# Two 2 MB stores of split weights become eight of 0.5 MB, moved from the attention of batch 0 to the steps beside the MoE block

## The chip, the cores and the metric

The kernel runs on one core of one Trainium2 chip. Time is device time in microseconds (us) of one execution, lower is better. The profile shown comes from one execution taken by the hardware profiler. The engines are PE (matrix multiply, with PEld for its weight loads), DVE (vector), ACT (scalar), POOL (GpSimd) and SP (sync). Two of them, SP and ACT, issue the DMA transfers here, each through a queue of its own: q1 in the profile is SP's, q10 is ACT's. Sixteen DMA engines carry the packets of both queues.

## The reference

Three stages run on x of shape (2, 768, 512), all in float32:

```python
# attention, B=2, H=8, S=768, D=64, with a mask from 6 hash bits
mask   = q_bucket[:, :, :, None] == k_bucket[:, :, None, :]
scores = where(mask, scale * q @ k.T, -1e9)
x      = softmax(scores) @ v                   # heads side by side: (2, 768, 512)
# gated block ("MoE")
h      = maximum(x @ w_in, 0);  u, v = h[..., :512], h[..., 512:]
v_n    = (v - mean(v)) / sqrt(var(v) + 1e-6)
v_s    = einsum('ts,bsd->btd', w_spatial, v_n) + b_spatial[None, :, None]
x      = (u * v_s) @ w_out
# channel block
xn     = (x - mean(x)) / sqrt(var(x) + 1e-6) * g_ln
out    = x + maximum(xn @ w_ch1, 0) @ w_ch2
```

`w_in`, `w_out`, `w_ch1` and `w_ch2` come as 64-bit floats and are converted on the chip. Float32 products are made of three passes over two parts, a rounded one and its remainder, so each weight is kept as a pair of arrays.

## The kernel before

The program is not written in the order in which it runs. Every operation is added to a list (class `Plan`). A planner then estimates a cost for each, lays them out by engine and by due time, and only then issues them. Each engine, and each queue of issued transfers, works in the order that came out of it. The line numbers in the profile are therefore almost all those of the one line that issues (L499); operations are told apart by their tiles.

**Attention.** There are 96 steps, one for each query tile of 128 rows: 2 batches x 8 heads x 6 tiles, so head 6 begins at step 36, head 8 (the first of batch 1) at step 48, head 10 at step 60, head 12 at step 72 and head 14 at step 84. A step makes scores (`sc`, PE), the masked maximum (`x<-sc`, DVE), the exponentials (`x<-x,nb`, ACT) and transposes (`pt`, PE, copied to `e`). After a head the weighted sum follows (`po`, 24 matmuls). The scores of a head read `ks`, which is put together from the split keys by five small transfers on SP's queue (`ks<-k` three times, `ks<-m` twice); `qs` is built in the same way for every three tiles. `ks` has two buffers, so that of one head is filled during the head before it.

**MoE block.** `moe1(0)` starts at step 60 (`M0`) and is spread over the steps to 96, 24 pieces in all; `moe1(1)` follows after the attention. The block's weights `v` and `u` (the two halves of `w_in`) and `out` are converted during the attention: `CONV_AT` gives the steps, four pieces of 0.5 MB for each weight. A piece is loaded (`f_v`, `f_u`, `f_out` on ACT's queue), turned from 64-bit words into a float on ACT, DVE and POOL, and split into the tile of its weight (2 MB, 16 KB a partition). The tiles of `v` and `u` stay on the chip until batch 0 of the block has used them. Then their room is taken, by `out` and by the second load of `v`. So both are also stored to `w_split` in memory, and read back for batch 1 by `reload` (`w_v<-ws_v`, `w_u<-ws_u`, SP). The stores run on ACT's queue. `out` is stored in eight pieces of 256 KB as it is split (`ws_out<-w_out`) and read by both batches.

**Later steps.** From step 71 on, eleven pieces of `w_ch1` are converted and kept in memory as well (`KEPT_AT`, tiles `f_w`, `f64c_w`, `kept`). Columns of `w_spatial` are loaded (`wst_sp`, SP) and split (`w_sp`) for the block's spatial product (`pg`), whose result, gated (`gt`) and transposed (`ptr_g`), goes into the product with `out` (`py`).

Functions in `conv_steps` are called with `plan.soon` set: the planner may place such an operation as soon as PE has come within 55 entries of it in the list, without regard to when it is due. Transfers are ordered by what they read and write, tile part by tile part, and the reuse of a tile waits for all that used it.

Of the kernel before, what the change touches and what calls it, by code (L numbers as in the profile page):

```python
# [9 lines left out]
F32 = mybir.dt.float32  # L10
# [494 lines left out]
def attn_moe_kernel(ctx: ExitStack, tc: tile.TileContext, qT, kT, v, proj, w_in, w_spT, b_sp, w_out, g_ln, w1, w2, out):  # L505
# [3 lines left out]
    nc = plan = Plan(tc)  # L509
# [15 lines left out]
    CB = 2  # L525
    CONV_AT = (5, 11, 18, 24, 31, 37, 44, 50, 58, 62, 66, 70)
    CONV_D = (-1, 0, 3, 3)
    KEPT = (6, 8, 10, 12, 14, 0, 1, 2, 3, 4, 5)
    KEPT_AT = (72, 75, 78, 81, 84, 86, 88, 90, 92, 94, 95)
    QA = 3  # L530
# [16 lines left out]
    KFT = DM // P  # L547
# [20 lines left out]
    def stage_f64(src, nm):  # L568
        a, n = src.shape[1], src.shape[2]
        st = pools["conv"].tile([P, a, n, 2], U32, tag="f64", name=f"f64_{nm}")  # L570
        nc.scalar.dma_start(out=st, in_=src)
        return st

    def words_f64(st, nm):

        a, n = st.shape[1], st.shape[2]
        lo, hi = st[:, :, :, 0], st[:, :, :, 1]
        c = pools["conv"].tile([P, a, n], U32, tag="f64c", name=f"f64c_{nm}")
        cf = c.bitcast(F32)
        nc.scalar.activation(cf, hi.bitcast(F32), AF.Abs)  # L580
        nc.vector.tensor_scalar(cf, cf, F64_MIN, F64_MAX, op0=ALU.max, op1=ALU.min)
        nc.vector.tensor_scalar(c, c, 3, 0x3FFFFFFF, op0=ALU.logical_shift_left, op1=ALU.bitwise_and)
        nc.vector.scalar_tensor_tensor(hi, hi, 0xC0000000, c, op0=ALU.bitwise_and, op1=ALU.bitwise_or)
        nc.vector.tensor_scalar(c, hi, 0xFF800000, None, op0=ALU.bitwise_and)
        nc.vector.scalar_tensor_tensor(cf, lo, 2.0**-52, cf, op0=ALU.mult, op1=ALU.mult)
        return hi.bitcast(F32), cf

    def join_f64(tf, cf):
        nc.gpsimd.tensor_tensor(cf, tf, cf, op=ALU.add)
        return cf  # L590
# [382 lines left out]
    w_split = {}  # L973
    wp = {}
    moe_w = []

    def converted(src, dst, nm, after=None):

        d = {}

        def stage():
            d["st"] = stage_f64(src, nm)

        def words():
            d["tc"] = words_f64(d["st"], nm)

        def join():
            d["f"] = join_f64(*d["tc"])

        def finish():  # L990
            to = dst()
            split_f64(to[0], to[1], d["f"].rearrange("p a n -> p (a n)"))
            after(to)

        return stage, words, join, finish

    def moe_tile(key, b):
        pool = mp if len(moe_w) % 2 else keep
        wp[key, b] = pool.tile([P, 2, KFT, HF], F32R, tag="w", name=f"w_{key}_{b}", bufs=1)
        moe_w.append(wp[key, b])  # L1000
        return wp[key, b]

    def conversions():

        res = []
        for key, src, at in (("v", w_in, HF), ("u", w_in, 0), ("out", w_out, 0)):
            w_split[key] = dram.tile([P, 2, KFT, HF], F32, tag=f"ws_{key}", name=f"ws_{key}")
            for k in range(KFT):

                def dst(key=key, k=k):  # L1010
                    if key == "out":
                        parts = [
                            mp.tile([P, NKT * P], F32R, tag=f"sp{i}", name=f"w_out_{k}_{i}", bufs=2 - i) for i in range(2)
                        ]
                        return [x[:, :HF] for x in parts]
                    if k == 0:
                        wp[key] = moe_tile(key, 0)
                    return [wp[key][:, i, k] for i in range(2)]

                def after(to, key=key, k=k):  # L1020
                    if key == "out":
                        for i in range(2):
                            nc.scalar.dma_start(out=w_split[key][:, i, k], in_=to[i].bitcast(F32))
                    elif k == KFT - 1:
                        nc.scalar.dma_start(out=w_split[key], in_=wp.pop(key).bitcast(F32))

                src_k = src[:, k : k + 1, at : at + HF]
                res.append(converted(src_k, dst, f"{key}_{k}", after))
        return res
# [152 lines left out]
    conv_steps = {}  # L1182
    for at, stages in zip(CONV_AT, convs):
        for delay, e in zip(CONV_D, stages):
            conv_steps.setdefault(at + delay, []).append(e)
    kept = {}
    for n, f in enumerate(KEPT):
        d = {}

        def kept_words(f=f, d=d):  # L1190
            d["tc"] = words_f64(d["st"], f"w1_{f}")

        def kept_join(f=f, d=d):
            kept[f] = dram.tile([P, KFT, P], F32, tag=f"kept{f}", name=f"kept_{f}")
            nc.scalar.dma_start(out=kept[f], in_=join_f64(*d["tc"]))

        def kept_stage(f=f, d=d):
            d["st"] = stage_f64(w1[:, :, f * P : (f + 1) * P], f"w1_{f}")

        for delay, e in zip(CONV_D, (kept_stage, kept_words, kept_join)):  # L1200
            conv_steps.setdefault(KEPT_AT[n] + delay, []).append(e)
    m0 = None
    n0 = 0
    for i in range(-1 - QA, NT + PO + 3):
# [449 lines left out]
```

## Time and profile before

| | |
|---|---|
| median of 3 runs | 660.97 us (659.72 to 661.21) |
| the profiled execution, own time | 658.13 us |
| its span, first to last instruction | 656.1 us |
| PE busy | 639.9 us (98%) |
| DVE, ACT, POOL busy | 503.1, 326.7, 218.1 us |
| mean granted TensorE clock | 0.995 |
| bytes moved by DMA | 107.68 MB in 60962 packets |

The span lies inside the execution's own time, with 2.0 us around it. PE is the engine with the most work. A time of one instruction in the timelines is its start and its length; square brackets give how long the engine stood idle before it and what ended that.

### The profile page before, as it was taken

The numbers are of one execution on the slowest core, as the hardware profiler recorded it, in microseconds if no ns is written. First come the engines' busy times: TensorE is split into PE (matmuls) and PEld (weight loads), VectorE is DVE, ScalarE is ACT, GpSimd is POOL, SyncE is SP. The second block draws the span as 40 slices with busy tenths as digits, with TensorE's granted clock in tenths as the row PEclk, the third lists the DMA queues.
The fourth block names the chain that finished last, engine by engine and source line by source line (L and its number), as shares of the span: only waits on it lengthen the run. The fifth ranks groups of instructions, "written<-read, shape, count | busy, mean of one in ns | idle before, by whom it ended". The sixth has DMA issues, their size and how long they took to land.

```text
span 656.1 us, 10066 instructions
## 1 busy us (share of the span) xinstructions
PE 639.9 (98%) x3506; PEld 523.8 (80%) x3506; DVE 503.1 (77%) x990; ACT 326.7 (50%) x650; POOL 218.1 (33%) x194
## 2 busy tenths in 40 slices
PE   7999979999999999999999999999999999999997
PEld 5777666666877867877788888899898988989896
DVE  6799847895788696677599635597998978989555
ACT  6888847776666654544375323372433342333110
POOL 2243423244455544222146200019624234232100
PEclk9999979999999999999999999999999999999999
DMA  6776874778357786473935113230355447271723
GB/s 156 201 198 149 265 170 136 179 254 224 97 178 207 226 220 179 136 254 124 333 105 201 57 56 120 87 108 19 118 185 208 147 150 252 78 273 35 251 83 145
DMA packets 60962, 107.68 MB, mean 164 GB/s; under 512 B 6816, under 2 KB 33136, under 8 KB 60144
## 3 DMA queue, kind: packets, MB, share of 16 engines
q1 hardware_dynamic: 43520, 71.78, 37.3%
q10 hardware_dynamic: 17392, 35.27, 16.2%
q8 instruction: 28, 0.46, 0.3%
q14 instruction: 22, 0.18, 0.1%
HBM read 63.31 MB, written 24.90 MB: 134 GB/s over the span
## 4 chain that ended last, share of the span: by engine, by line
PE 88%; issue 3%; DMA 3%; DVE 2%; ACT 2%; SPq 1%; POOL 0%; ACTq 0%; POOLq 0%
PE acc L499 20%; PE p L499 13%; PE pv L499 10%; PE sc L499 9%; PE pt L499 8%; PE po L499 8%; PE pg L499 7%; PE pc L499 5%; PE py L499 5%; ACT x L499 1%; DMA ks<-k 1%; SPq L499 1%; PE px_c L499 1%; PE ptr_g L499 1%; PE pz L499 1%
## 5 line engine op out<-in xcount | busy, mean ns | idle before, releaser
L499 PE MATMUL acc<-w,ch 128*128 128x512 f32 x576 | 142.7, 392 | 0.0
L499 PEld LDWEIGHTS acc<-w,ch 128*128 128x128 f32 x576 | 107.3, 188 | 19.1
L499 DVE TENSOR_SCALAR_CACHE_REDUCE x<-sc 128x768 f32<-128x768 f32 x96 | 90.5, 951 | 18.9 <-PE sc L499 10.3
L499 ACT ACTIVATE x<-x,nb 128x768 f32<-128x768 f32 x96 | 89.9, 937 | 26.7 <-DVE x L499 25.9
L499 PE MATMUL sc<-ks,qs 128*128 128x512 f32 (+3 forms) x384 | 94.7, 368 | 7.1 <-issue 4.0
L499 POOL TENSOR_TENSOR f64c_w<-f_w,f64c_w 128x512 f32<-128x512 f32 x32 | 45.2, 1412 | 124.9 <-issue 70.3
L499 PE MATMUL pt<-ident,x 128*128 128x128 f32 x576 | 82.0, 277 | 0.9 <-DVE gt L499 0.6
L499 PEld LDWEIGHTS sc<-ks,qs 128*128 128x128 f32 (+1 forms) x384 | 65.4, 194 | 20.9 <-issue 7.3
L499 PEld LDWEIGHTS pt<-ident,x 128*128 128x128 f32 x576 | 67.3, 142 | 14.0 <-issue 3.6
L499 ACT ACTIVATE e<-pt 128x384 f32<-128x384 f32 x120 | 55.9, 487 | 32.4 <-PE pt L499 32.1
L499 PE MATMUL po<-e,vv 128*64 128x384 f32 x384 | 65.5, 490 | 0.2 <-DVE e L499 0.2
L499 ACT ACTIVATE ch<-u 128x384 fp32r<-128x384 f32 x48 | 25.1, 527 | 74.5 <-DVE u L499 72.9
L499 DVE TENSOR_TENSOR u<-p,u 128x384 f32<-128x384 f32 x84 | 45.0, 549 | 17.4 <-PE p L499 17.1
L499 PEld LDWEIGHTS po<-e,vv 128*64 128x64 f32 x384 | 26.1, 137 | 31.7 <-issue 29.7
L499 PE MATMUL p<-t,w 128*128 128x384 f32 x252 | 50.3, 338 | 0.0
L499 PE MATMUL p<-xh,w 128*128 128x384 f32 x252 | 49.1, 338 | 0.7 <-DVE u L499 0.7
L499 DVE COPY e<-pt 128x384 f32<-128x384 f32 x72 | 39.5, 552 | 10.9 <-PE pt L499 10.7
L499 PEld LDWEIGHTS p<-xh,w 128*128 128x128 f32 x252 | 44.7, 188 | 2.9 <-DVE u L499 1.0
L499 PEld LDWEIGHTS p<-t,w 128*128 128x128 f32 x252 | 44.8, 188 | 2.3 <-DVE u L499 0.2
L499 POOL TENSOR_TENSOR w<-f64c_w,w 128x512 fp32r<-128x512 f32 (+1 forms) x28 | 37.8, 1355 | 20.7 <-ACT w L499 18.4
L499 PE MATMUL pg<-vn,w_sp 128*128 128x512 f32 x180 | 43.8, 397 | 0.6 <-ACT e L499 0.6
L499 DVE TENSOR_SCALAR f64c_w<-f64c_w 128x512 f32<-128x512 f32 x64 | 34.6, 540 | 12.3 <-ACT f64c_w L499 10.5
(156 smaller groups left out, 1043.9 us busy)
## 6 DMA issues: line engine op xcount, KB each, us to landing
f_w<-in_w ACTq DMA_DIRECT2D x32, 512.0 KB
ots<-y_dram SPq DMA_DIRECT2D x12, 768.0 KB
ks<-k SPq DMA_DIRECT2D x45, 192.0 KB
y_dram<-ots SPq DMA_DIRECT2D x30, 256.0 KB
qs<-q SPq DMA_DIRECT2D x30, 192.0 KB
wst_sp<-in_w_spT SPq DMA_DIRECT2D x12, 384.0 KB
w_out<-ws_out SPq DMA_DIRECT2D x2, 2048.0 KB
vv<-in_v SPq DMA_DIRECT2D x16, 192.0 KB
```

The source lines that it names most:

```text
L499: getattr(getattr(nc, engine[j.engine]), op)(*map(live, args), **{k: live(x) for k, x in kw.items()})
```

## The change

The two stores of 2 MB (`v` at step 27, `u` at step 53) are taken out. In their place each weight's four pieces (`k` = 0 to 3, 0.5 MB each) are stored by separate transfers, still on ACT's queue, at the steps of `STORE_AT`: those of `v` at 61, 64, 67 and 70, those of `u` at 73, 76, 79 and 82. A piece has two runs of 2 KB in each of 128 partitions, one for each part of the split.

```diff
     CONV_D = (-1, 0, 3, 3)
+    STORE_AT = (61, 64, 67, 70, 73, 76, 79, 82)
...
                         for i in range(2):
                             nc.scalar.dma_start(out=w_split[key][:, i, k], in_=to[i].bitcast(F32))
-                    elif k == KFT - 1:
-                        nc.scalar.dma_start(out=w_split[key], in_=wp.pop(key).bitcast(F32))
...
             conv_steps.setdefault(KEPT_AT[n] + delay, []).append(e)
+    for n, (key, k) in enumerate((key, k) for key in "vu" for k in range(KFT)):
+
+        def store(key=key, k=k):
+            nc.scalar.dma_start(out=w_split[key][:, :, k], in_=wp[key, 0][:, :, k].bitcast(F32))
+
+        conv_steps.setdefault(STORE_AT[n], []).append(store)
```

## Rows read from the trace of the kernel before

**Rows 1.** The page: busy time by engine, and the span in 40 slices.
```profile
PE 639.9 (98%) x3506; PEld 523.8 (80%) x3506; DVE 503.1 (77%) x990; ACT 326.7 (50%) x650; POOL 218.1 (33%) x194
...
PE   7999979999999999999999999999999999999997
...
PEclk9999979999999999999999999999999999999999
```

**Rows 2.** PE's waits, whole span: us in total, times, longest.
```profile
PE sc L499 <- issue: 4.0, 1, 4.0
...
PE sc L499 <- DMA ks<-k: 1.4, 1, 1.4
```

**Rows 3.** Timeline of PE around two heads' first scores.
```profile
85.84 0.49 PE L499 MATMUL pt<-ident,x 128*128 128x128 f32 x3
90.31 1.62 PE L499 MATMUL sc<-ks,qs 128*128 128x512 f32 x4 [3.98 <-issue]
...
150.13 0.95 PE L499 MATMUL sc<-ks,qs 128*128 128x512 f32 x4 [1.40 <-DMA ks<-k]
```

**Rows 4.** Timeline of ACT's and SP's queues: start and length of the issuing instruction.
```profile
77.21 0.34 ACTq L499 DMA_DIRECT2D ws_v<-w_v  x1
81.48 1.81 SPq L499 DMA_DIRECT2D ks<-k  x1
83.34 1.04 SPq L499 DMA_DIRECT2D ks<-m  x1
...
139.60 0.70 ACTq L499 DMA_DIRECT2D ws_u<-w_u  x1
...
145.83 1.76 SPq L499 DMA_DIRECT2D ks<-m  x1
```

**Rows 5.** DMA by queue, 78 to 83 us: packets, MB, share of 16 engines.
```profile
q10 hardware_dynamic: 128, 2.10, 102.3%
q1 hardware_dynamic: 36, 0.04, 2.8%
```

**Rows 6.** DMA by queue, 83.5 to 90.5 us.
```profile
q1 hardware_dynamic: 682, 1.01, 72.5%
```

**Rows 7.** DMA by queue, 142.8 to 148.3 us.
```profile
q10 hardware_dynamic: 170, 2.12, 90.3%
q1 hardware_dynamic: 105, 0.19, 9.0%
```

**Rows 8.** Windows: length, busy us (instructions) by engine, clock, DMA share, GB/s.
```profile
20.00:80.00 60.00, 59.65 (x407) 43.20 (x405) 52.33 (x108) 49.48 (x111) 24.76 (x23) 1.00 0.72 195
...
86.30:90.30 4.00, 0.03 (x1) 0.02 (x1) 0.84 (x3) 1.76 (x5) 1.26 (x1) 0.97 1.04 207
90.30:96.90 6.60, 6.59 (x25) 6.09 (x26) 2.62 (x7) 2.77 (x6) 0.72 (x2) 0.50 0.37 87
```

**Rows 9.** The chain that ended last, 70 to 115 us: start, length, what.
```profile
78.01 0.71 PE sc L499 x4
78.72 0.66 PE pt L499 x6
...
92.57 1.28 PE sc L499 x4
...
95.77 1.27 PE pt L499 x6
```

**Rows 10.** Timelines: SP's issue for head 8, and its first scores on PE.
```profile
117.70 0.78 SPq L499 DMA_DIRECT2D ks<-m  x1
...
121.78 1.42 PE L499 MATMUL sc<-ks,qs 128*128 128x512 f32 x6
```

**Rows 11.** DMA, 189 to 191.3 us: one 256 KB store of out, alone.
```profile
DMA packets 144, 0.26 MB, mean 114 GB/s; under 512 B 16, under 2 KB 16, under 8 KB 144
...
q10 hardware_dynamic: 144, 0.26, 30.2%
```

**Rows 12.** DMA by queue, 160 to 163.6 us: stores of out beside SP's transfers.
```profile
q1 hardware_dynamic: 387, 0.85, 66.8%
q10 hardware_dynamic: 195, 0.34, 24.9%
```

**Rows 13.** Windows of the steps beside the MoE block.
```profile
150.00:240.00 90.00, 89.87 (x523) 68.59 (x524) 69.69 (x147) 53.54 (x108) 45.17 (x39) 1.00 0.69 192
212.90:219.90 7.00, 7.00 (x40) 6.00 (x39) 5.24 (x13) 4.86 (x10) 3.82 (x4) 1.00 0.90 318
240.00:245.00 5.00, 3.77 (x22) 2.92 (x21) 4.97 (x11) 3.10 (x8) 1.29 (x1) 1.00 0.72 173
```

**Rows 14.** Timeline of SP's queue and PE: w_out's load, head 14, second load of v.
```profile
212.02 0.34 SPq L499 DMA_DIRECT2D w_out<-ws_out  x1
...
232.56 0.47 SPq L499 DMA_DIRECT2D ks<-k  x1
...
242.02 0.98 PE L499 MATMUL sc<-ks,qs 128*128 128x512 f32 x4
...
280.27 0.42 SPq L499 DMA_DIRECT2D w_v<-ws_v  x1
```

## The prediction

> **What bounds the kernel now.** I read the page first, to find the engine that sets the time. It is PE: busy 98% of the span, against 77% of DVE, 50% of ACT and 33% of POOL [rows 1]. So a change pays only by giving PE less to do, less to wait for, or a faster clock. The slices say where to look. Beyond the first and the last, one slice alone shows PE under nine tenths, the sixth (82 to 98 us), and the clock is low in the same slice and nowhere else [rows 1]. The list of PE's waits names two on transfers in the middle of the kernel: 4.0 us once and 1.4 us once, both before scores (`sc`) [rows 2]. The timeline puts them at 86.3 to 90.31 us, before the first scores of head 6, and just ahead of 150.13 us, before those of head 10 [rows 3]. For the second the profile names the load of `ks`. For the first it has no name ("issue"), so I looked at the queues.
>
> There the two stores appear. That of `v` is issued at 77.21 us, that of `u` at 139.60 us, each a few us ahead of the last transfers for a `ks`: at 81.48 and 83.34 us for head 6, at 145.83 us for head 10 [rows 4]. The view of DMA by queue then shows what happened between issue and use. From 78 to 83 us the store's queue took all of the sixteen engines (102.3%, which is 128 packets of 16 KB), and SP's queue 2.8% [rows 5]. In the next 7 us SP's queue works off what had gathered, at 72.5% [rows 6], and PE stands until it comes to `ks`. The second store does the same from 142.8 to 148.3 us: 90.3% against 9.0% [rows 7]. So a store of 2 MB holds up SP's small transfers by its own length: 1.023 x 5.0 = 5.1 us for `v`, 0.903 x 5.5 = 5.0 us for `u`.
>
> **What the removal gives.** Three terms.
>
> *The wait at head 6, 3.98 us* [rows 3]. Without the store its `ks` would be there 5.1 us sooner, at about 85.2 us, ahead of the 86.33 us at which PE ran out. A bound from the other side: head 8, with no store near it, starts its scores 4.08 us after the last issue for its `ks`, and does not wait (117.70 to 121.78 us) [rows 10]. Put on head 6's last issue, 83.34 us, that gives 87.42 us, a wait of 1.1 us that stays. But the issues themselves were stretched (1.81 us for one `ks<-k`) [rows 4], so they would come earlier too. I keep 0.3 us and take 3.7.
>
> *The clock, 3.3 us.* From 90.3 to 96.9 us the granted clock is 0.50, 1.2 in place of 2.4 GHz, after PE had stood; PE is busy for 6.59 of the 6.60 us [rows 8]. Four `sc` matmuls take 1.28 us there and 0.71 at full clock, six transposes 1.27 and 0.66 [rows 9]. The factor is 1.8 to 1.9. The stretch at full clock is 6.6 / 1.9 = 3.4 us, so 3.2 us are given back; counting the 12 `sc` and 12 transposes of the chain by rows 9 (2.13 + 1.32 = 3.45 against 6.73) gives 3.3. DVE and ACT have 2.62 and 2.77 us of work in it, less than 3.4 [rows 8], so they don't take PE's place as the limit. If 1.1 us of the wait stayed, the clock would still be saved: after the wait of 1.40 us at head 10 the clock was 1.00 [rows 3, 8, 13].
>
> *The wait at head 10, 1.40 us* [rows 3]. 5.0 us sooner, its `ks` would be in time. By head 8's 4.08 us on the issue at 145.83 us, 149.91 us, almost all of it would stay. I take 1.2.
>
> Sum 3.7 + 3.3 + 1.2 = 8.2 us; between 6.4 (both bounds against it: 2.9 + 3.3 + 0.2) and 8.7. It is kept to the end because the stretch behind is PE's: 59.65 of 60 us busy in the like steps [rows 8], 89.87 of 90 after head 10 [rows 13].
>
> **What the new stores cost.** Steps 60 to 84 run from 150.13 to 242.02 us [rows 3, 14], 3.8 us a step; the stores follow each other every 3 steps, 11.5 us, from about 154 us to 234, or some steps sooner, since they are called with `soon`.
>
> *Issuing.* Six more issues of 0.34 us on ACT [rows 4]: 2 us, beside an ACT that is busy 53.54 of 90 us there [rows 13]. What they read was written long before, so they hold nothing up behind them. Cost 0.
>
> *Transfer.* The nearest row is a store of `out`, 256 KB in 128 packets of 2 KB (and 16 tiny ones): 30.2% of 2.3 us, 0.69 us of the sixteen engines [rows 11]. A piece of 0.5 MB is 1.4 us, the eight 11.1, against 10.1 for the two now. The engines' share in those 90 us rises from 0.69 [rows 13] by 11.1 / 90 = 0.12, to 0.81. What a piece can hold up is 1.4 us at a time, and less if the queues take turns: with stores of `out` in flight SP's queue got 66.8% and they 24.9% [rows 12], far from the 2.8% beside packets of 16 KB.
>
> The Trainium skill speaks against small pieces: "DMA: Bandwidth & Descriptors", section Bandwidth, asks for 1 MiB or more a transfer, and its section on the anatomy of one DMA gives about 2 us fixed plus bytes over 436 GB/s. That would be an estimated 8 x 3.2 = 26 us of transfers one after another against 2 x 6.8 = 14, 12 us more of ACT's queue. Both are given there for another issuing path, and rows 11 show 0.69 us of engine time for half such a piece. By the page the sum for PE would not change as long as no instruction of PE waits for these stores.
>
> *Who waits.* Nobody soon. The reuse of `v`'s tile by `out` starts at 212.02 us, of `u`'s tile at 280.27 us [rows 14], after steps 70 (188 us) and 82 (234 us). Behind a piece on ACT's queue stand loads of `f_out` and `f_w`; on the engines beside it, `ks`, `qs` and `wst_sp`. Head 14's `ks` is issued 9.5 us ahead of its scores [rows 14], against head 8's 4.08, so 5 us are spare. The nearest trial in this stretch is the load of `w_out`: 2 MB at once, 0.90 of all engines for 7 us, on SP's own queue, and PE was busy 7.00 of 7.00 us [rows 13, 14]. From below 0, then, and from above the whole 11.1 us, were PE to pay for each transfer. I take 0.5 us, near the trial: PE already loses 1.23 us from 240 to 245 us, with DVE full at 4.97 of 5 [rows 13], and what comes late there is not covered.
>
> **The sum.** 8.2 - 0.5 = 7.7 us less. On the profiled execution that is 658.13 - 7.7 = 650.4 us (span 656.1 to 648.4). That execution is 2.84 us below the median of the runs and outside their spread, so the timed figure goes from the median: 660.97 - 7.7 = 653.3 us. A gain or loss of 0.2%, 1.3 us, is about what can be told from none here.
>
> **Rivals.**
>
> *Half of it.* The small transfers are late without the store as well, or the planner, which orders all operations anew from its costs, sets the new order so that one wait of two us or so returns. For it: head 8 has no store near it and starts on the last 4 us. Against it: 5.1 us of delay are taken away and only 3.98 were waited. Gain 2 to 6 us, 655 to 659 us. Chance 0.20.
>
> *It moves the wait.* One head beside the MoE block gets its `ks` as late as head 6 did, and pays wait and clock: 4.0 + 3.3 = 7.3. Gain 0.9, about 660 us, no difference. Against it: pieces of 1.4 us and 5 us spare at head 14. Chance 0.07.
>
> *PE pays for every piece (slower).* ACT runs in order; if a piece ahead of an `f_out` or `f_w` load makes the conversion late, ACT waits in front of the exponentials, and PE behind it. Eight times 1.4 us is 11.1, net 8.2 - 11.1, about 664 us. It decides from 8.2 / 8 = 1.0 us a piece. For it: DMA is busy 0.69 there and DVE full in places. Against it: PE's 7.00 of 7.00 beside the 2 MB load. With a store that lands earlier than its step and adds to head 10's wait, chance 0.12.
>
> **Chances and range.** The forecast, a gain of 6 to 9 us (652 to 655), has 0.61. Faster 0.61 + 0.20, less a little at the edge, 0.80; same 0.08; slower 0.12. The upper end takes in the second case, 659 us. The lower end takes the full 8.7 us from the profiled execution, 649.4, rounded to 649.5. Out of it are most of the two cases without gain.
>
> **What would show it.** Right: no store of 2 MB on q10 between 70 and 150 us; PE's wait before head 6's first scores gone or under 1.1 us; no low clock after the start; no wait at head 10; span up to head 10 some 8 us shorter, and the rest as long as before. Wrong: a wait of over 2 us before a head's first scores anywhere, the clock low again, or waits of PE on `pg` or `sc` from 150 to 250 us behind late `f_w`, `wst_sp` or `ks`.

## The result, and the profile after

Six runs of the changed kernel have a median of 652.41 us (650.54 to 653.30); six of the kernel before, 659.62 us (658.26 to 661.21). The ratio is 0.9883, with an interval of 0.986 to 0.9905: 7.2 us faster, where 7.7 was forecast and 653.3 us named. The profiled execution of the changed kernel took 653.30 us, the longest of its six, with a span of 651.5 us. One run of experiment 9 (1283.23 us) and one of experiment 11 (757.39 us) lie far above all others of their kernels and are left out of the figures below.

The page of the changed kernel: span, busy time by engine, the 40 slices.

```profile
span 651.5 us, 10061 instructions
...
PE 639.1 (98%) x3506; PEld 521.7 (80%) x3506; DVE 507.9 (78%) x990; ACT 325.4 (50%) x650; POOL 212.2 (33%) x194
...
PE   8899999999999999999999999999999999999997
...
PEclk9899999999999999999999999999999999999999
```

Against [rows 1] PE's work is the same to a us, and the bytes are the same 107.68 MB: what went is idle and slow time. The sixth slice is full in both lines. But the second one is not: 8 for PE and 8 for the clock, where the kernel before has 9 and 9. PE's waits name it; this is the longest of the whole span:

```profile
PE pm L499 <- DMA k<-in_kT: 2.8, 1, 2.8
```

Both waits of [rows 2] are gone, and a new one of 2.8 us stands ahead of the hash products (`pm`), from the load of `k`. The timeline of PE, with the first scores of heads 2, 6, 10 and 14:

```profile
24.59 0.52 PE L499 MATMUL pm<-k,sides 128*32 128x384 f32 x2 [2.77 <-DMA k<-in_kT]
...
36.18 0.95 PE L499 MATMUL sc<-ks,qs 128*128 128x512 f32 x4
...
90.62 0.96 PE L499 MATMUL sc<-ks,qs 128*128 128x512 f32 x4
...
144.55 0.96 PE L499 MATMUL sc<-ks,qs 128*128 128x512 f32 x4
...
236.40 0.96 PE L499 MATMUL sc<-ks,qs 128*128 128x512 f32 x4
```

In the kernel before head 2 began here:

```profile
32.41 0.83 PE L499 MATMUL sc<-ks,qs 128*128 128x512 f32 x3
```

So the changed kernel is 3.8 us late there. Then it gains: from head 2 to head 10 it takes 108.4 us where the kernel before took 117.7 (150.13 in [rows 3]), 9.3 us less. From head 10 to head 14 it is 91.85 against 91.89 us (242.02 in [rows 14]). From head 14 to the end of the span it is 415.1 against 414.1. The sum, 3.8 - 9.3 - 0.04 + 1.0, is the 4.6 us by which this pair of spans differs. Up to head 10 the span is 5.6 us shorter, where the forecast named some 8.

The windows of the changed kernel (columns as in [rows 8]): the start, its low clock, the stretch of head 6, the stretch of the new stores.

```profile
18.00:37.00 19.00, 16.23 (x104) 11.95 (x102) 12.62 (x24) 12.34 (x28) 4.32 (x4) 0.91 0.62 154
25.90:29.30 3.40, 3.40 (x15) 2.91 (x13) 2.90 (x5) 1.44 (x4) 2.32 (x2) 0.50 0.59 127
66.00:90.30 24.30, 24.30 (x168) 17.12 (x167) 20.17 (x44) 18.93 (x44) 9.15 (x9) 1.00 0.67 166
...
150.00:240.00 90.00, 89.27 (x519) 67.80 (x518) 74.41 (x152) 53.94 (x110) 42.77 (x38) 1.00 0.81 240
```

Around head 6 PE is busy for all of 24.30 us at full clock. In the 90 us of the stores the DMA share went from 0.69 [rows 13] to 0.81. Two pieces of `v` in flight show how the queues shared the engines, issues first, then DMA by queue from 150 to 162 us:

```profile
150.49 0.60 ACTq L499 DMA_DIRECT2D ws_v<-w_v  x1
...
155.98 0.56 ACTq L499 DMA_DIRECT2D ws_v<-w_v  x1
```

```profile
q10 hardware_dynamic: 976, 2.10, 48.3%
q1 hardware_dynamic: 774, 1.43, 42.1%
```

That is another picture than the 102.3% against 2.8% of [rows 5].

What made the start late is in the timelines of the two queues. The first load for a weight, `f_v`, is issued 0.28 us ahead of the load of `k` that PE comes to wait for; before, it was issued at 23.24 us, 5.7 us behind that load.

```profile
16.02 0.35 ACTq L499 DMA_DIRECT2D f_v<-in_w_in  x1
...
16.30 0.33 SPq L499 DMA_DIRECT2D k<-in_kT  x1
```

No line of the diff moves that load. The planner lays out all operations anew, and moved it.

The low clock at the start belongs to the profiled run alone. Its 3.4 us at half clock, with 1.0 us of tail, bring that run's mean clock down to 0.997; the five other runs have 0.998 to 1.000, too much for such a stretch. Whether they have the wait is not recorded.

### The profile page after: what moved, and what is told of

It reads as the page before. It is cut to its first block, busy times and chain, and to the rows that moved or that the text cites. A ratio compares the mean times of both kernels' runs of the same rounds, so it can differ in the third digit from the quotient of the medians.

```text
span 651.5 us, 10061 instructions
## 1 busy us (share of the span) xinstructions
PE 639.1 (98%) x3506; PEld 521.7 (80%) x3506; DVE 507.9 (78%) x990; ACT 325.4 (50%) x650; POOL 212.2 (33%) x194
## 2 busy tenths in 40 slices
DMA packets 62850, 107.68 MB, mean 165 GB/s; under 512 B 6912, under 2 KB 33232, under 8 KB 62288
## 4 chain that ended last, share of the span: by engine, by line
PE 87%; DVE 6%; DMA 3%; ACT 1%; issue 1%; POOL 0%; ACTq 0%; DVEq 0%; POOLq 0%
PE acc L499 20%; PE p L499 14%; PE po L499 9%; PE sc L499 8%; PE pv L499 8%; PE pt L499 8%; PE pg L499 7%; PE pc L499 5%; PE py L499 5%; DVE x L499 2%; DMA f_w<-in_w 2%; DMA k<-in_kT 1%; PE pm L499 1%; PE warm L499 1%; PE ptr_g L499 1%
## 5 line engine op out<-in xcount | busy, mean ns | idle before, releaser
L499 PEld LDWEIGHTS sc<-ks,qs 128*128 128x128 f32 (+1 forms) x384 | 63.7, 192 | 13.5 <-issue 3.0
L499 POOL TENSOR_TENSOR w<-f64c_w,w 128x512 fp32r<-128x512 f32 (+1 forms) x28 | 35.2, 1257 | 32.5 <-ACT w L499 28.4
```

Of the source, the lines that this page charges most:

```text
L499: getattr(getattr(nc, engine[j.engine]), op)(*map(live, args), **{k: live(x) for k, x in kw.items()})
```

## The experiments

The theory after the result (A): the gain is the two stores taken out of the way of small transfers, and the planner's new order costs 3 to 4 us at the start. The rivals: (B) the new order is the gain, and where the stores stand matters little; (C) it is the size of the packets, not the place; (D) the stores cost something in their new place that the gain hides.

To hold the order still, the planner goes on planning the old transfer, which is then not issued, and the transfers under test are issued on ACT's queue just ahead of the first scores of a named step. All other operations of every engine and queue keep their order. The core of that edit:

```diff
-                for op, args, kw in j.calls:
+                op, args, kw = j.calls[0]
+                for put, src in self.before.pop(getattr(getattr(args[0], "base", None), "name", None), ()) if j.engine == "PE" else ():
+                    nc.scalar.dma_start(out=live(put), in_=live(src))
+                for op, args, kw in () if j.ghost else j.calls:
```

`put_pieces("v", (63, 64, 67, 70))` below issues the four pieces of `v` so, `put_whole("v", 32)` the store of 2 MB. The issuing line is L504, or L502 for a transfer issued in this way. The kernel before was timed beside each: its median is 659.82 us beside experiments 1 to 4, 659.10 beside 5 to 8 and 658.93 beside 9 to 11, and each of these groups ran on a chip of its own. A ratio is always to the kernel before of the same group, with its interval in brackets. Differences from version 3 (experiment 3) are told between medians; by the ratios and their intervals, one of less than some 2 us can't be told from none.

**1. The order of before, with eight late pieces.** On the kernel before:

```diff
+    put_pieces("v", (63, 64, 67, 70))
+    put_pieces("u", (73, 76, 80, 82))
```

> The order of the kernel before on every engine and queue, with only the two stores of 2 MB taken out of ACT's order and the eight pieces put in where the changed kernel has them (just ahead of the scores of steps 63, 64, 67, 70 and 73, 76, 80, 82). Theory A (the big stores held up SP's small transfers, and their removal is the whole gain): 659.6 - (3.98 + 3.3 + 1.4) = about 651 us, no wait of PE at heads 6 and 10, the clock full from the start to the tail; 1 to 2 us below the changed kernel, since the wait at 21.8 us for a load of k isn't in this order. Theory B (the gain comes from the new order that the planner writes): about 659.5 us, as before.

653.15 us (651.83 to 654.17) against 659.82: ratio 0.9897 (0.9875 to 0.9919), 6.7 us faster, 2 us short of A's figure. With the order held, the stores alone bring nearly the whole gain, and B falls for the order of before. Its profile has full clock up to the tail; PE's timeline at the first scores of heads 5 to 10 (head 9 by a view of its own):

```profile
72.86 0.95 PE L504 MATMUL sc<-ks,qs 128*128 128x512 f32 x4
...
86.58 0.96 PE L504 MATMUL sc<-ks,qs 128*128 128x512 f32 x4
...
102.31 0.95 PE L504 MATMUL sc<-ks,qs 128*128 128x512 f32 x4
...
117.66 1.53 PE L504 MATMUL sc<-ks,qs 128*128 128x512 f32 x6 [1.88 <-issue]
...
131.68 0.50 PE L504 MATMUL sc<-ks,qs 128*128 128x512 f32 x1 [0.21 <-DVE x L504]
...
145.48 0.96 PE L504 MATMUL sc<-ks,qs 128*128 128x512 f32 x4
```

In the kernel before, heads 5, 7 and 9 began here (6, 8 and 10: [rows 3, 10]):

```profile
72.36 0.95 PE L499 MATMUL sc<-ks,qs 128*128 128x512 f32 x4
...
108.53 0.95 PE L499 MATMUL sc<-ks,qs 128*128 128x512 f32 x4
...
134.69 0.50 PE L499 MATMUL sc<-ks,qs 128*128 128x512 f32 x1
```

From head to head, with the order unchanged: 5 to 6 took 13.7 us in place of 17.9, 6 to 7 15.7 in place of 18.2, 9 to 10 13.8 in place of 15.4. That is 4.2 + 2.5 + 1.6 = 8.3 us. Heads 7 to 9 gave 3.2 of it back, 1.88 of them in the wait above, and head 5 began 0.5 us later, so that head 10 begins 4.65 us sooner in this pair of profiles. At head 8 a load of `f_u` (0.5 MB) is issued at 111.12 us, just ahead of the transfers for `ks` at 111.61: with less to wait for earlier on, the two came together (experiment 11 takes them apart again).

**2. The order of after, with two whole stores.** On the changed kernel:

```diff
+    put_whole("v", 32)
+    put_whole("u", 63)
```

> The order of the changed kernel with the eight pieces taken out and the two stores of 2 MB put in, v ahead of the scores of step 32 as in the kernel before, u ahead of step 63 (it isn't ready sooner in this order). Theory A: SP's transfers for head 6 come some 5 us later; in this order they land 2 us ahead of need, so a wait of about 3 us at head 6 and, where the clock falls after it, 3 us more: 655.5 to 659 us. The store of u stands after head 10's transfers here and costs nothing. Theory B: 652.4 us, as the changed kernel.

652.29 us (651.50 to 654.93), ratio 0.9895 (0.9871 to 0.9919): as fast as the changed kernel. That is B's figure, and a miss for A as it then stood. The profile, of the longest of the six runs, shows for `v` a wait of PE for `qs` within head 5 and low clock behind it, but nothing for `u`, whose 2 MB leave at 155.05 us. PE's timeline, then windows:

```profile
82.55 0.70 PE L504 MATMUL sc<-ks,qs 128*128 128x512 f32 x2 [1.76 <-DMA qs<-q]
```

```profile
84.00:88.00 4.00, 4.00 (x16) 1.54 (x16) 3.60 (x8) 2.21 (x5) 0.00 (x0) 0.57 0.78 186
150.00:240.00 90.00, 90.00 (x525) 68.67 (x526) 76.23 (x154) 54.83 (x111) 45.57 (x40) 1.00 0.76 217
```

So a whole store is not costly everywhere, and in this order even that of `v` cost less than before: the profile's mean clock is 0.996, but the five other runs have 0.999 or 1.000, too much for a low stretch of 3.4 us. Besides, the wait at the start is 2.0 us here with no low clock, and head 2 begins at 34.38 us, 1.8 us sooner than in the profile of the changed kernel, with the same order up to there. The start blurs the comparison, and the later experiments take it out first.

**3. The changed kernel, with the first load of `f_v` later.** Issued ahead of the scores of step 8, which makes it 18.82 us (23.24 in the kernel before):

```diff
+            plan.ghost = nm == "v_0"
...
+            if nm == "v_0":
+                b, h, g, j = order[8]
+                plan.before[f"sc_{b}_{h}_{g}_{j}"] = [(d["st"], src)]
```

> The changed kernel, with one issue moved in ACT's order: the first load of f_v goes out just ahead of the scores of step 8, as in the kernel before, in place of 16.0 us. Theory A' (the new order costs time at the start, because this 0.5 MB load runs beside the load of k that PE waits for): the wait of 2.8 us goes, and the low clock where it followed: 648.5 to 650 us. Rival (the load of k is late by its own place in SP's order, or PE loses the time again a few us on): 652 us.

649.12 us (648.34 to 651.31), ratio 0.9849 (0.9822 to 0.9875): 10.7 us faster than before and 3.3 us faster than the changed kernel; the fastest version measured. By the means of the six runs the step from the changed kernel is 2.4 us, and the intervals of the two ratios overlap a little, so its size is rough. The issue, PE's hash products, and the windows of the start and of the stores:

```profile
18.82 0.36 ACTq L502 DMA_DIRECT2D f_v<-in_w_in  x1
...
21.76 0.52 PE L504 MATMUL pm<-k,sides 128*32 128x384 f32 x2
```

```profile
18.00:37.00 19.00, 18.94 (x134) 14.40 (x132) 16.67 (x37) 16.53 (x38) 4.84 (x4) 1.00 0.75 197
...
150.00:240.00 90.00, 90.00 (x520) 68.40 (x519) 75.17 (x151) 54.23 (x108) 41.98 (x38) 1.00 0.83 240
```

One load issued 2.8 us later takes the wait and the low clock away. PE is busy for 18.94 of 19 us where the changed kernel had 16.23. This version ("version 3") is the base of the experiments 5 to 10.

**4. The order of before, each store cut into four pieces issued back to back at its old place.**

```diff
-    put_pieces("v", (63, 64, 67, 70))
-    put_pieces("u", (73, 76, 80, 82))
+    put_pieces("v", (33, 33, 33, 33))
+    put_pieces("u", (57, 57, 57, 57))
```

> The order of the kernel before, with each store of 2 MB cut into its four pieces, issued back to back at the old place: the same bytes at the same time, in packets of 2 KB in place of 16 KB. If the place is what counts (SP's queue loses the engines for the length of the bytes, whatever their form): 659.5 us, wait of 4 us and low clock at head 6. If the packet size is what counts (queues take turns packet by packet, so small packets leave SP half of the engines): the wait at head 6 falls to 1 or 2 us or nothing, 651 to 656 us.

668.82 us (667.08 to 671.38), ratio 1.0142 (1.0116 to 1.0168): 9 us slower than before, outside both figures. C falls: the same 2 KB packets that do no harm late do more than the 16 KB packets did here. DMA by queue (on q10 a load of `f_u` follows the four pieces) from 79.7 to 88.5 us, and PE's timeline behind it:

```profile
q10 hardware_dynamic: 1128, 2.26, 78.6%
q1 hardware_dynamic: 311, 0.48, 24.5%
```

```profile
90.11 0.47 PE L504 MATMUL sc<-ks,qs 128*128 128x512 f32 x1 [2.14 <-DMA ws_v<-w_v]
...
94.03 1.19 PE L504 MATMUL sc<-ks,qs 76*128 76x512 f32 x3 [3.45 <-DMA ks<-m]
```

SP's queue got a fourth of the engines in place of 2.8%, but for 8.8 us, and PE stood twice. Behind each of the two bursts the clock is low for 6.8 us (from 92.5 and from 157.4 us); before there was one such stretch.

**5. Version 3, with `v` whole at step 32** (the pieces of `u` stay): `put_whole("v", 32)`.

> The changed order with the first f_v load late (649.1 us, no wait at the start), and in it v alone stored whole, 2 MB, ahead of step 32 as in the kernel before; u stays in four pieces. Theory A (a 2 MB store among the attention heads of batch 0 holds up SP's transfers, in any order): in the run with both stores whole this order lost 3.7 us at heads 5 and 6 in the profiled execution; so 652 to 655 us, with waits of PE on qs or ks between 78 and 95 us. Rival (in the changed order there is enough slack, and the loss seen there was that one execution's): 649 us, 0 to 1 us.

650.95 us (649.72 to 653.86), ratio 0.9886 (0.9866 to 0.9906): 1.8 us above version 3 (2.4 by the ratios), between the two theories. PE waits once in the profile, and the clock stays full:

```profile
88.28 0.74 PE L504 MATMUL sc<-ks,qs 76*128 76x512 f32 x3 [1.39 <-DMA ks<-m]
```

The store leaves at 74.27 us here, 9.9 us ahead of the last issue for head 6's `ks` (84.17 us), where the kernel before had 6.1 (77.21 to 83.34 in [rows 4]): that fits a price that hangs on what is due right behind the store. Why experiment 2 is as fast as the changed kernel is not shown: this small price of `v`, and a start that differs between runs, could make it up.

**6. Version 3, without any store of `v` and `u`.** The planned stores aren't issued, and the second loads read the stored `out` instead, so batch 1 of the block works with other weights.

> The same order, late f_v load, and no store of v or u at all: the second load of both reads the stored out weight in their place (so the gated block of batch 1 uses other weights). It prices the eight pieces. Theory A (pieces cost PE nothing): 649.1 us, within 0.6. Rival (each piece costs up to its 1.4 us): 8 x 1.4 = 11 us less at most, 638 to 646 us; my own figure of 0.5 us can hardly be told from nothing.

649.98 us (649.47 to 651.47, 4 runs), ratio 0.9865 (0.985 to 0.988), against 649.12 with the stores. D falls: by the two intervals, a cost of the eight pieces over 1 us is out; the forecast's 0.5 can't be told from nothing. In the profiled pair this version's span is 1.2 us longer, and that stands ahead of every store: ten warm-up matmuls take 2.40 us in place of 1.31 and head 1 begins at 10.34 us, not 8.92. From head 1 to the end of the span it takes 638.1 us, version 3 638.3. The window of the stores, without them:

```profile
150.00:240.00 90.00, 90.00 (x523) 68.62 (x522) 76.85 (x151) 55.06 (x109) 43.10 (x38) 1.00 0.69 194
```

**7. Version 3, with a second copy of every piece**: `put_pieces` at the steps of experiment 1, into other memory.

> The same order, late f_v load, and each of the eight pieces stored twice, the second copy to memory that nobody reads: 4 MB more of stores in the same steps. Theory A (the steps beside the gated block have room): 649 to 650.5 us. Rival (the room is used up by the first copies): 11 us of engine time more, 652 us or above, with waits of PE on pg, pt or sc from 150 to 250 us.

654.61 us (654.59 to 656.31, 5 runs), ratio 0.9937 (0.9923 to 0.9951): 5.5 us above version 3: a miss for A, and the rival's figure. Yet it is no price for each piece. Heads 10 to 13 take 70.6 us as in version 3, heads 13 to 14 25.2 in place of 20.4, by one wait of PE with 3.4 us of low clock, behind one of ACT for a load of `f_w`:

```profile
220.71 0.66 ACT L504 ACTIVATE f64c_w<-f_w 128x512 f32<-128x512 f32 x1 [7.21 <-DMA f_w<-in_w]
...
PE pt L504 <- ACT xT L504: 3.4, 1, 3.4
```

**8. Version 3, with both stores whole and late**: `put_whole("v", 67)`, `put_whole("u", 76)`.

> The same order, late f_v load, v and u each stored whole, 2 MB in packets of 16 KB, but beside the gated block: v ahead of step 67, u ahead of step 76. It tells the place from the cutting. If the place is what gains: 649 to 650 us, no wait of PE. If the cutting is needed there: SP's transfers are held 5 us each time, and a wait of 2 to 5 us comes at head 12 or 13 or at pg, 652 to 656 us.

658.17 us (657.05 to 659.84, 11 runs), ratio 0.9988 (0.9978 to 0.9997): 9.0 us above version 3, more than either figure. That of `v` cost nothing: heads 11 to 13 take 48.5 us with it and without. That of `u` cost it all (heads 13 to 14: 29.9 us in place of 20.4). The timelines of ACT's queue, ACT and PE, then the window of the low clock:

```profile
206.87 0.33 ACTq L502 DMA_DIRECT2D ws_u<-w_u  x1
...
207.32 0.46 ACTq L504 DMA_DIRECT2D f_w<-in_w  x1
...
224.22 0.66 ACT L504 ACTIVATE f64c_w<-f_w 128x512 f32<-128x512 f32 x1 [10.99 <-DMA ks<-k]
...
226.34 0.90 PE L504 MATMUL pt<-ident,x 128*128 128x128 f32 x3 [7.20 <-ACT xT L504]
```

```profile
221.40:231.70 10.30, 5.36 (x22) 4.75 (x22) 5.08 (x10) 6.19 (x12) 1.91 (x1) 0.50 0.59 155
```

This is the mechanism of the forecast's slower rival, at one place. The load of `f_w` stands on ACT's queue behind the store, both share the engines with the 2 MB of `w_out` on SP's queue (issued at 205.19 us), and ACT waits in order for `f_w` in front of what PE needs. (The profile names `ks<-k` for ACT's wait, which is the transfer that landed last; the instruction reads `f_w`, whose last packets end at 222.80 us.) The changed kernel has the same wait, smaller, and experiment 7 lies between:

```profile
220.33 0.67 ACT L499 ACTIVATE f64c_w<-f_w 128x512 f32<-128x512 f32 x1 [4.54 <-DMA f_w<-in_w]
...
222.45 0.93 PE L499 MATMUL pt<-ident,x 128*128 128x128 f32 x6 [0.73 <-ACT xT L499]
```

ACT 4.54 and PE 0.73 us in the changed kernel, 7.21 and 3.40 in experiment 7, 10.99 and 7.20 here: each time PE waits 3.8 us less than ACT. Below 3.8 us it waits for nothing (version 3: ACT 3.70, PE 0).

**9. As 8, with `u` three steps sooner**, ahead of `w_out`'s load: `put_whole("u", 73)` in place of 76.

> As the run with both weights stored whole beside the gated block, but u three steps sooner: ahead of step 73 in place of 76, so that its 2 MB are through before the load of w_out begins; v ahead of 67 as there. In that run PE waited at one place alone, 7.2 us, where ACT stood for an f_w load that was queued behind the store of u while w_out was loaded. Theory A2 (what costs is two bulk transfers within the same few us ahead of something that is due soon, whatever their form): no such wait, 649 to 650.5 us. Rival (in packets of 16 KB a store beside the block costs wherever it stands): a wait of 3 us or more somewhere from 150 to 250 us, 653 us or above.

652.26 us (649.37 to 654.06, 5 runs), ratio 0.99 (0.9869 to 0.9932), in two groups: 649.37 and 649.97, as A2 has it, and 652.26, 653.98 and 654.06, near the rival's figure. The profile is of the 649.97: the store leaves at 192.58 us, 14.5 us ahead of that load, ACT waits 1.16 us for `f_w`, and PE is busy for 89.58 of 90 us. So without the collision the whole stores can cost nothing; the longer runs have a mean clock of 0.997 in place of 1.000, so something stalls in them, and no profile shows what. Whether 14.5 us of distance are enough stays open.

**10. Version 3, with all eight pieces spread over batch 0**: `put_pieces("v", (19, 22, 26, 33))`, `put_pieces("u", (39, 46, 54, 63))`.

> The changed order with the late f_v load, and the eight pieces stored one by one soon after each is split, mostly during the attention of batch 0: v ahead of steps 19, 22, 26 and 33, u ahead of 39, 46, 54 and 63. Theory A2 (the burst is what costs, not batch 0 as a place): 1.4 us of engines at a time is within the 1 to 2 us by which transfers for a head land early, so 649 to 651 us. Rival (batch 0 has no room for any store): up to 1.4 us for each of seven, and low clock where a wait is long, 653 to 660 us.

650.20 us (649.25 to 652.39), ratio 0.9869 (0.9847 to 0.9892), with full clock and no wait over 0.5 us of PE for a transfer. It is A2's figure. The 1.1 us above version 3 are less than the times can tell. In the profiled pair the span is 1.0 us longer, and that stands ahead of every store: head 1 begins 1.3 us later, and from there to the end of the span it takes 638.0 us, version 3 638.3. So in this order it is not the attention of batch 0 that the stores had to leave. Pieces spread there in the order of before were not tried.

**11. Experiment 1, with the last load of `f_u` issued ahead of head 8's scores**, out of the way of head 8's `ks`:

```diff
+            plan.ghost = nm == "u_3"
...
+                b, h, g, j = order[48]
+                plan.before[f"sc_{b}_{h}_{g}_{j}"] = [(d["st"], src)]
```

> The order of the kernel before with the eight late pieces, as in the first run, and the last f_u load (0.5 MB) issued a few places later in ACT's order, ahead of head 8's first scores. In the first run PE waited 1.9 us at head 8, behind that load: all had moved up by 7 us except that its issue now came half a microsecond ahead of SP's transfers for head 8. If that wait is what kept the gain at 6.7 in place of the 8.2 us of the forecast: 650.5 to 652 us, no wait at head 8. If something else did: 653 us.

653.34 us (652.55 to 655.25, 5 runs), ratio 0.9918 (0.9895 to 0.9941): no gain over experiment 1, a miss. The wait at head 8 is gone, and PE is there 1.9 us sooner (115.78 us, not 117.66), but stalls at head 14 in its place. PE's timeline there, and the window behind it:

```profile
236.58 0.55 PE L504 MATMUL pt<-ident,x 128*128 128x128 f32 x3 [1.07 <-DVE gt L504]
```

```profile
238.80:242.30 3.50, 3.26 (x8) 2.61 (x9) 3.15 (x7) 3.50 (x8) 0.00 (x0) 0.51 1.04 261
```

## Why the prediction was right, point by point

**The two waits and the clock: right, together and nearly one by one.** Forecast 3.7 + 3.3 + 1.2 = 8.2 us; experiment 1, whose order is that of before, shows 4.2 + 2.5 + 1.6 = 8.3 in the three stretches, and the changed kernel 9.3 from head 2 to head 10. That it would be "kept to the end" was too much: experiment 1 gave 3.2 of it back in heads 7 to 9. The two remainders that the forecast kept back by head 8's 4.08 us [rows 10] did not come: both waits went whole, since the issues were no longer stretched. The clock term was too big by 0.8 us. Its 6.73 us is the chain's own time, with 1.62 us for the first scores; by the 1.28 and 1.27 us of [rows 9] alone, the 12 scores and 12 transposes take 6.38, which gives 2.9 back in place of 3.3. The forecast also compared the work of DVE and ACT in the stretch with PE's (2.62 and 2.77 us against 3.4) and took them out as limits. But work is also waited for in turn: in experiment 1 the chain that ended last runs through DVE and ACT here, and PE stands 0.42 us for ACT's `e`. The chain of experiment 1, then PE's timeline:

```profile
88.94 0.98 DVE x L504 x2
...
90.00 1.03 ACT x L504 x2
91.04 0.38 ACT e L504
```

```profile
91.46 0.93 PE L504 MATMUL pt<-ident,x 128*128 128x128 f32 x6 [0.42 <-ACT e L504]
```

From head 6 to head 7 PE's busy time fell by 2.7 us, and its idle time, beside the wait that went, rose by 0.2.

**The new stores: 0.5 us forecast, none found.** Version 3 has them, experiment 6 has not, and the times are 649.12 and 649.98. The transfer was sized well: the share of 0.81 was forecast and found. One piece of `u`, issued at 195.82 us in the changed kernel, has ACT's queue to itself; DMA by queue from 196 to 200 us:

```profile
q10 hardware_dynamic: 272, 0.52, 34.8%
```

That is 0.348 x 4.0 = 1.4 us of the sixteen engines, as forecast from [rows 11]. From the issue to the end of its last packet (198.51 us) it took 2.7 us. The Trainium skill ("DMA: Bandwidth & Descriptors", the section on the anatomy of one DMA) gives, for another issuing path, an estimated 3.2 us for a whole transfer of this size, its completion included; the 2.7 us, without the completion, don't speak against it. The same page's section Bandwidth advises 1 MiB or more a transfer for what the transfer itself reaches; here the 2 MB transfer was the costly one, for what waited beside it.

**The slower rival: its mechanism is there, with 3.8 us to spare.** ACT does wait in order behind an `f_w` load, and in the changed kernel PE loses 0.73 us by it. The forecast looked at head 14's `ks` and at w_out's load [rows 13, 14] each by itself; where that load, a store and `f_w` meet, ACT waits 4.54 us and all of the 3.8 us that were spare are used. With twice the pieces (experiment 7), or a whole store 1.7 us behind `w_out`'s load (experiment 8), the rival's mechanism costs 5.5 and 9.0 us.

**What failed: the start.** The sum has no term for what the planner does elsewhere. The forecast named the new order only in the rival "half of it", as a wait before a head, and said of the profile to come that no low clock would stand after the start; the profiled run has one from 25.9 us, which its list counts as a sign of being wrong. The wait came at 21.8 to 24.6 us, before any store of either kernel, for a load moved beside another: 3.3 us between the medians of the changed kernel and version 3, 4.4 us at head 2 in the two profiles. So 7.2 beside 7.7 is in part luck. The sum came out near because the terms were on the cautious side, the removal in the profiled pair being 1.1 us and the stores 0.5 us better than forecast, and because the timed runs lost less than the profiled one: the forecast of 7.7 met 7.2 timed, but 4.6 us in the pair of spans.

**The explanation, mended.** The forecast took the length of the packets (16 KB) and the place as the two reasons. Experiment 4 takes away the first and is slower; experiment 10 takes away the second, in the changed order, and is as fast as the late pieces within 1.1 us. What costs, as far as these runs go, is the burst: 2 MB within 5 to 9 us ahead of transfers that are due (before, 4, 8, in part 5). The same bytes in pieces some steps apart cost nothing that could be told in either place (3 against 6, 10), and whole stores cost nothing where no transfer is due soon (2 for `u`, 8 for `v`). The order counts as well: where it puts 9.9 us between the whole store of `v` and the last transfer for head 6, the store costs some 2 us (5); where it puts 6.1, the wait and the low clock at head 6 cost 4.2 + 2.5 us (before against 1). Left open is which of the two, the cutting or the later place, is needed in the order of before (experiment 1 has both); so are the longer runs of experiment 9, and how far the wait at the start differs between runs of the changed kernel.

## What to carry to other kernels

Where one queue moves bulk and another the small transfers that the next step waits for, look at DMA by queue in the few us between the issue of the small one and its use: here a bulk transfer was harmless or not by what was due behind it, not by its size or its packets alone, and spread in pieces it cost nothing that could be told. With a planner that orders all anew, compare the issue times of transfers far from the change too, and undo each that moved ahead of one that PE waits for; here that one load was worth some 3 us, beside the 7.2 that the change had brought. Before adding work beside a wait that costs nothing, take the slack from the trace (how long may ACT wait until PE does?), as a wait of 4.5 us was nearly free and one of 11 us cost 9.

## What the runs showed of the hardware

Queues did not share the DMA engines by halves, nor by one rule that the packets' size gives. Beside a store of 16 KB packets SP's queue had 2.8% for 5 us [rows 5], but 17.6% (experiment 5, 75 to 81 us) and 22.8% (experiment 2, 77 to 83 us) beside the same store in the changed order. Beside four stores in 2 KB packets back to back it had 24.5% for 8.8 us (experiment 4); beside two such stores 5.5 us apart, with pieces of `out` and a load on the same queue, 42.1% against 48.3% (after). SP moved 0.48 MB in the stretch of experiment 4 and 0.04 in that of [rows 5], so these shares also tell what SP's queue had to send.

The length of one wait does not tell whether the clock falls. It fell after waits of PE of 2.77 us (after, the start), 1.76 (experiment 2), 3.40 (7), 3.98 (before) and 7.20 (8), and after 1.07 us with others near it (11). It stayed at 2.4 GHz after 1.39 us (5), 1.40 (before, head 10), 1.88 (1) and 2.0 us (2, the start).
